# Retention followed by a gated feed-forward: Y, S and the next A in one block on TensorE, even pairs prepared sooner

## The chip, the core and the metric

The kernel runs on one core of one Trainium2 chip. The metric is the time of one execution on the device in microseconds (us). Before the change it is 210.73 us, the median of 4 runs (210.41 to 212.07).

## The reference

A linear recurrence ("retention") with a decay for each head feeds a two-layer network whose middle function is h·cos(h):

```python
# batch 4, heads 8, sequence 768, head size 64; gamma[h] = 1 - 2**(-5-h)
for t in range(S):
    state = gamma * state + outer(k[:, :, t], v[:, :, t])     # 64 x 64 per batch and head
    y[:, :, t] = (1 / sqrt(D)) * q[:, :, t] @ state
x = y as 3072 rows of 512
h = x @ w_in            # 512 x 2048
out = (h * cos(h)) @ w_out   # 2048 x 512, out is 3072 x 512 float32
```

## The kernel before

**Pairs and groups.** The sequence is cut into 6 chunks of 128 positions, and two batch rows are worked on together. One chunk of two batch rows is a "pair" `p`, numbered 0 to 11; pairs 0 to 5 are the first two batch rows, pairs 6 to 11 the other two, and at pairs 0 and 6 the state starts anew. Two neighbouring pairs make a "group" `g` of 512 rows, numbered 0 to 5, on which the feed-forward works.

**Steps of a pair.**

- Loads: six DMAs of 256 KB (q, k and v for each of the two batch rows, float32), issued from GpSimd's queue (L131), with some early ones on SyncE's.
- Conversion to bf16 with the decay multiplied in: q and v on GpSimd (`conv_q` L181, `conv_v` L186), k as a plain copy on ScalarE (`conv_k` L192). The function `ahead(p)` emits all three.
- Transposes of q and k: for the first pairs on TensorE (`stage_t`), from pair 4 on by two DMA transposes on SyncE's queue (`stage_t_dma` L218), written into the tile `qkt`.
- A (`stage_a` L235): for each batch row 8 matmuls of 64 rows by 128 columns, so 16 a pair; the products k·q go into four PSUM banks, two for each batch row.
- M (`stage_m` L244): VectorE multiplies these four banks by the causal mask and writes the tile `am`, four instructions, two for each batch row.
- Y (`half_y`, one call for each batch row): matmuls of the state from before (`stb`, L257; left out at pairs 0 and 6) and of `vs` with `am` (L262) into one bank for each batch row. ScalarE copies each bank into `xt` (L266).
- S (`stage_s` L279): 16 matmuls that add the pair's own part to the state in the PSUM tile `st_ps`. Then two copies bring the state to SBUF as `stb` for the next pair (L284; on VectorE from pair 4 on). Pairs 5 and 11 have no S.

**Steps of a group.** F is `unit_f` (L310): 4 matmuls of 128x512 against `w_in` give one of 16 slices of h; ScalarE takes the cosine (L299, tile `cosb`), VectorE multiplies it in (L303, tile `gt`), and then the bank is free. O is `unit_o` (L334): 4 of the 16 matmuls against `w_out` for one 128-row slice of the output; after the fourth such part ScalarE copies the bank to `ob` (L341) and SyncE's queue sends it out (L342).

**What sets the order.** Everything is emitted in an order that is written out by hand, and each engine executes its own instructions in that order. PSUM has 8 banks: one is `st_ps`, the other seven are handed out by `Banks`. A small model (`Clock`) guesses when each bank is free, and the bank with the earliest guess is taken; the actual wait is by semaphore. From group 2 on, the loop over `g` has 16 slots `s`; each has one F of group `g` and, for `g` above 2, one O of group `g - 1`. In group 2 six O of group 1 are interleaved (slots 0, 2, 4, 6, 8, 10). Beside these, a slot emits steps of the pairs of group `g + 1`, with r = s mod 8 and p = 2(g+1) for the first eight slots and 2(g+1)+1 for the others: the conversions of pair p+1 at r = 0, its DMA transposes at r = 1, A of pair p with half of M at r = 2, the other half of M at r = 3, and at r = 6 Y, S and the state copies of pair p and the loads of pair p+3.

The tiles `qk`, `vs` and `qkt` have three buffers each (pair modulo 3), `stb`, `am`, `xt` and `gt` have two.

Of the kernel before, what the change touches and what calls it, by code (L numbers as in the profile page):

```python
# [47 lines left out]
def kernel(  # L48
# [9 lines left out]
    nc = tc.nc  # L58
    B, H, S, D = q.shape
    C = 128  # L60
    NC = S // C
# [5 lines left out]
    NP = B // 2 * NC  # L67
    NG = NP // 2
# [15 lines left out]
    clk = Clock()  # L84
# [41 lines left out]
    def load(eng, p, names):  # L126
        bp, c = divmod(p, NC)
        for n in names:
            t, src = SRC[n[0]]
            b = int(n[1])  # L130
            eng.dma_start(  # L131
                out=t[SLOT[p]][b],
                in_=src[2 * bp + b, :, ds(c * C, C)].rearrange("h t d -> t h d"))
# [45 lines left out]
    def conv_q(p, eng, bs=(0, 1)):  # L179
        for b in bs:  # L180
            eng.tensor_tensor(out=qk[p % NB][:, b, 0], in0=qf[SLOT[p]][b],  # L181
                              in1=bc(gq, p % NC), op=ALU.mult)

    def conv_v(p, eng, bs=(0, 1), g=None):
        for b in bs:
            eng.tensor_tensor(out=vs[p % NB][:, b], in0=vf[SLOT[p]][b],  # L186
                              in1=bc(gk if g is None else g, p % NC), op=ALU.mult)

    def conv_k(p, on_act):
        for b in range(2):  # L190
            if on_act:
                nc.scalar.copy(out=qk[p % NB][:, b, 1], in_=kf[SLOT[p]][b])  # L192
                clk.run("act", 0.6)
            else:
                nc.vector.tensor_copy(out=qk[p % NB][:, b, 1], in_=kf[SLOT[p]][b])
# [19 lines left out]
    def stage_t_dma(p):  # L215
        n = p % NB
        for b in range(2):
            nc.sync.dma_start_transpose(  # L218
                out=qkt[n][:, b].rearrange("p w a t -> p (w a) t"),
                in_=qk[n][:, b].rearrange("p w h d -> p (w h d)"))  # L220

    def qt(n, b, a):
        return qkt[n][:, b, 0, a, :]

    def kt(n, b, a):
        return qkt[n][:, b, 1, a, :]

    def stage_a(p, b):
        n = p % NB
        bk = [banks.take(), banks.take()]  # L230
        ap = [t.rearrange("p (a t) -> p a t", a=HP) for t in bk]
        for a in range(HP):
            for j in range(2):
                po = 64 * j
                nc.tensor.matmul(ap[j][:, a, :], lhsT=kt(n, b, a)[po : po + 64, :],  # L235
                                 rhs=qt(n, b, a)[po : po + 64, :],
                                 tile_position=(po, 0))
        clk.run("pe", 0.3)
        return b, bk, ap, clk.pe

    def stage_m(p, item, parts=(0, 1)):
        b, bk, ap, done = item
        for j in parts:
            nc.vector.tensor_tensor(  # L244
                out=am[p % 2][b][j], in0=ap[j],
                in1=mask.unsqueeze(1).to_broadcast([128, HP, 128]), op=ALU.mult)
            banks.give(bk[j], clk.run("dve", 0.64, done + 0.1))

    def half_y(p, b):
        c = p % NC  # L250
        n = p % NB
        bank = banks.take()
        yp = bank.rearrange("p (a t) -> p a t", a=HP)
        for a in range(HP):
            if c > 0:
                for j in range(2):
                    nc.tensor.matmul(  # L257
                        yp[ts(j, 64), a, :], lhsT=stb[p % 2][:, b, a, ts(j, 64)],
                        rhs=qt(n, b, a), start=True, stop=False,
                        skip_group_check=True)  # L260
            for j in range(2):
                nc.tensor.matmul(  # L262
                    yp[ts(j, 64), a, :], lhsT=vs[n][:, b, 2 * a + j, :],
                    rhs=am[p % 2][b][j][:, a, :], start=(c == 0), stop=True,
                    skip_group_check=True)
        nc.scalar.copy(out=xt[(p // 2) % 2][:, :, ts(2 * (p % 2) + b, C)], in_=yp)  # L266
        clk.run("pe", 0.5)
        banks.give(bank, clk.run("act", 0.6, clk.pe + 0.1))

    def stage_s(p, copy_st):  # L270
        c = p % NC
        n = p % NB
        if c == NC - 1:
            return
        for b in range(2):
            for a in range(HP):
                for j in range(2):
                    h = 2 * a + j
                    nc.tensor.matmul(  # L279
                        st_ps[ts(j, 64), b, a, :], lhsT=qk[n][:, b, 1, h, :],  # L280
                        rhs=vs[n][:, b, h, :], start=(c == 0 and b == 0 and a == 0),
                        stop=True, skip_group_check=True)
        for j in range(2):
            copy_st(out=stb[(p + 1) % 2][ts(j, 64), :, :, ts(j, 64)], in_=st_ps[ts(j, 64)])  # L284
            clk.run("act" if copy_st == nc.scalar.copy else "dve", 0.65, clk.pe + 0.3)
        clk.run("pe", 0.25)

    def stage_y(p, copy_st=nc.vector.tensor_copy):
        for b in range(2):
            half_y(p, b)  # L290
        stage_s(p, copy_st)
# [15 lines left out]
    def unit_f(g, f):  # L307
        bank = banks.take()
        for i in range(KIN):
            nc.tensor.matmul(bank, lhsT=w_in_t(i, f), rhs=xt[g % 2][:, i, :],  # L310
                             start=(i == 0), stop=(i == KIN - 1))
        banks.give(bank, act(bank, gt[g % 2][:, f, :]))
# [16 lines left out]
    def unit_o(g, j, part):  # L329
        if part == 0:  # L330
            o_bank[j] = banks.take()
        bank = o_bank[j]
        for f in range(4 * part, 4 * part + 4):
            nc.tensor.matmul(bank, lhsT=gt[g % 2][:, f, ts(j, 128)], rhs=w_out_sb[:, f, :],  # L334
                             start=(f == 0), stop=(f == KOUT - 1))
        clk.run("pe", 0.87)
        if part == 3:
            o = ob[j % 4]
            bp, c = divmod(2 * g + j // 2, NC)
            dst = out[ds((2 * bp + j % 2) * S + c * C, C), :]  # L340
            nc.scalar.copy(out=o, in_=bank)  # L341
            nc.sync.dma_start(out=dst, in_=o)  # L342
            banks.give(bank, clk.run("act", 0.6, clk.pe + 0.1))
# [27 lines left out]
    def attend(p):  # L371
        for it in [stage_a(p, b) for b in range(2)]:
            stage_m(p, it)
# [36 lines left out]
    stage_t(1, 1)  # L410
    warm(1)
    stage_s(0, nc.scalar.copy)
    a10 = stage_a(1, 0)
    stage_m(1, a10)
# [6 lines left out]
    pair_f(0, 0, (0,))  # L421
    half_y(1, 1)
    stage_s(1, nc.scalar.copy)
    pair_f(0, 0, (1,))
    pair_f(1, 0)
# [56 lines left out]
    def ahead(p):  # L482
        if p < NP:
            conv_q(p, nc.gpsimd)
            conv_k(p, True)
            conv_v(p, nc.gpsimd)

    def later(p):
        stage_y(p)
        n = 8 if p == 4 else p + 3 if p > 5 else NP  # L490
        if n < NP:
            load(nc.gpsimd, n, ("q0", "k0", "q1", "k1", "v0", "v1"))

    def o_units(g, a, b):
        for u in range(a, b):
            unit_o(g, *divmod(u, 4))

    o_units(1, 0, 2)
    attend(4)
    stage_t_dma(6)  # L500
    o_units(1, 2, 6)
    later(4)
    attend(5)
    o_units(1, 6, 10)
    later(5)

    for g in range(2, NG + 1):
        for s in range(16):
            hf, r = divmod(s, 8)
            p = 2 * (g + 1) + hf  # L510
            if g == 2 and s % 2 == 0 and s < 12:
                unit_o(1, *divmod(10 + s // 2, 4))
            if g < NG:
                unit_f(g, s)
            if g > 2:
                if g < NG or s < 12:
                    unit_o(g - 1, *divmod(s, 4))
                elif s == 12:
                    last_o(g - 1, 3)
            if p < NP:  # L520
                if r == 0:
                    ahead(p + 1)
                elif r == 1:
                    if p + 1 < NP:
                        stage_t_dma(p + 1)
                elif r == 2:
                    todo = [stage_a(p, b) for b in range(2)]
                    stage_m(p, todo[0])
                elif r == 3:
                    stage_m(p, todo[1])  # L530
                elif r == 6:
                    later(p)


# [28 lines left out]
```

## Time and profile before

| What | Value |
|---|---|
| median of 4 runs | 210.73 us (210.41 to 212.07) |
| the profiled execution | 210.85 us, of which the span from first to last instruction is 209.1 us |
| TensorE matmul busy | 199.8 us, 1648 instructions |
| VectorE busy | 113.9 us, 189 instructions |
| ScalarE busy | 113.1 us, 189 instructions |
| GpSimd busy | 101.8 us, 117 instructions |
| granted TensorE clock | 1.000 |
| DMA | 33.83 MB, mean 162 GB/s |

The profile names engines PE (TensorE matmuls), PEld (TensorE weight loads), DVE (VectorE), ACT (ScalarE), POOL (GpSimd) and SP (SyncE); a q behind the name means the engine's queue of instructions that do no arithmetic, DMA issues among them. A row of the timeline or of the chain gives a start in us from the span's beginning, a length in us, the engine, the line in the kernel, the operation and how many instructions were merged into the row. Some matmul records are missing from a trace, so a row may say x15 or x3 where the program has 16 or 4; spaces of time between starts are then the better measure than counts. "Busy" on PE is the time from a matmul's start to its modelled end, and neighbouring matmuls overlap.

### The profile page before, as it was taken

Reading aid. Unit: us, or ns where it says so; the run is one execution under the profiler, and the core shown is the slowest. Engines: PE = TensorE matmul, PEld = TensorE weight load, DVE = VectorE, ACT = ScalarE, POOL = GpSimd, SP = SyncE. Lnnn points to the kernel's source line nnn. Section 1 sums busy time; section 2 is a strip of 40 time slices with the busy share of each in tenths; the row PEclk is TensorE's granted clock in tenths of the full one; section 3 lists DMA queues with packets and bytes.
Section 4 is the critical chain, followed back from the end, with each engine's and each line's share of the span. In section 5 each row is a group of like instructions: output and inputs, shape, how many; then the busy total and the mean of one; then the engine's idle time right before and its main releaser. Section 6 shows DMA issues by size and latency. Waiting matters only on the chain.

```text
span 209.1 us, 4209 instructions
## 1 busy us (share of the span) xinstructions
PE 199.8 (96%) x1648; PEld 115.6 (55%) x1671; DVE 113.9 (54%) x189; ACT 113.1 (54%) x189; POOL 101.8 (49%) x117
## 2 busy tenths in 40 slices
PE   7679999999999999999999999999999999999993
PEld 3258854558897555555545445545545444444452
DVE  5674885542967472968874575565565233333000
ACT  6386874237898227477744744734544654553120
POOL 7998238399999999999994130000000000000000
PEclk9999999999999999999999999999999999999999
DMA  6999999999999999959999991141101101110212
GB/s 153 332 251 207 216 252 288 330 261 285 274 301 240 262 263 269 223 183 215 149 250 110 137 202 50 56 100 50 53 0 50 50 3 50 50 52 6 97 63 87
DMA packets 37604, 33.83 MB, mean 162 GB/s; under 512 B 27792, under 2 KB 30096, under 8 KB 37584
## 3 DMA queue, kind: packets, MB, share of 16 engines
q0 software_dynamic: 7728, 20.71, 39.0%
q1 hardware_dynamic: 29712, 12.75, 27.9%
q8 instruction: 13, 0.21, 0.4%
q10 hardware_dynamic: 144, 0.10, 0.1%
q14 instruction: 7, 0.06, 0.1%
HBM read 27.26 MB, written 6.29 MB: 160 GB/s over the span
## 4 chain that ended last, share of the span: by engine, by line
PE 91%; DMA 3%; ACT 2%; issue 1%; SPq 1%; DVE 0%; DVEq 0%; ACTq 0%
PE bank L334 38%; PE bank L310 30%; PE bank L321 10%; DMA qf<-in_q_dram 3%; PE bank L235 3%; PE bank L257 3%; PE bank L262 3%; PE bank L351 2%; PE st_ps L279 1%; PE bank L208 1%; SPq L131 1%; ACT qk L391 1%; PE bank L368 1%; ACT qk L192 0%; ACT xt L266 0%
## 5 line engine op out<-in xcount | busy, mean ns | idle before, releaser
L303 DVE TENSOR_TENSOR gt<-bank,cosb 128x512 bf16<-128x512 f32 x96 | 65.2, 689 | 62.7 <-ACT cosb L299 62.5
L299 ACT ACTIVATE cosb<-bank,halfpi 128x512 bf16<-128x512 f32 x96 | 65.5, 687 | 50.5 <-PE bank L310 45.7
L334 PE MATMUL bank<-w_out_sb,gt 128*128 128x512 bf16 x358 | 88.4, 379 | 0.7 <-issue 0.3
L310 PE MATMUL bank<-xt,w_in 128*128 128x512 bf16 x277 | 70.4, 380 | 1.2 <-issue 0.9
L334 PEld LDWEIGHTS <-gt 128*128 128x128 bf16 x368 | 35.5, 98 | 41.2
L310 PEld LDWEIGHTS <-w_in 128*128 128x128 bf16 x288 | 31.8, 114 | 28.4
L244 DVE TENSOR_TENSOR am<-bank,mask 128x512 bf16<-128x512 f32 x48 | 30.3, 681 | 1.6 <-PE bank L235 1.5
L186 POOL TENSOR_TENSOR vs<-vf,gk 128x512 bf16<-128x512 f32 x22 | 22.5, 1045 | 3.5 <-DMA vf<-in_v_dram 3.5
L341 ACT COPY ob<-bank 128x512 f32<-128x512 f32 x23 | 13.4, 586 | 19.3 <-PE bank L334 19.2
L131 POOL DMA_DIRECT2D vf<-in_v_dram x23 | 20.3, 887 | 4.9 <-DMA w_out_sb<-in_moe_w_out_dram 4.9
L181 POOL TENSOR_TENSOR qk<-qf,gq 128x512 bf16<-128x512 f32 x18 | 18.5, 1050 | 7.7 <-issue 4.8
L321 PE MATMUL bank<-xt,w_in 128*128 128x256 bf16 x192 | 22.0, 273 | 0.0
L131 POOL DMA_DIRECT2D kf<-in_k_dram x23 | 20.6, 897 | 2.1 <-DMA w_out_sb<-in_moe_w_out_dram 1.2
L321 PEld LDWEIGHTS <-w_in 128*128 128x128 bf16 x192 | 20.7, 114 | 0.5
L192 ACT CAST qk<-kf 128x512 bf16<-128x512 f32 x24 | 13.7, 613 | 8.1 <-DMA kf<-in_k_dram 8.1
L266 ACT CAST xt<-bank 128x512 bf16<-128x512 f32 x24 | 13.0, 586 | 7.5 <-PE bank L262 7.5
L131 POOL DMA_DIRECT2D qf<-in_q_dram x17 | 15.3, 901 | 1.6 <-DMA w_in<-in_moe_w_in_dram 1.6
L262 PE MATMUL bank<-am,vs 128*64 128x128 bf16 x192 | 11.9, 220 | 0.6 <-POOL vs L186 0.6
L257 PEld LDWEIGHTS <-stb 128*64 128x64 bf16 x160 | 8.7, 109 | 4.4 <-issue 3.3
L262 PEld LDWEIGHTS <-vs 128*64 128x64 bf16 x192 | 10.0, 110 | 2.0 <-POOL vs L186 1.6
L284 DVE CAST stb<-st_ps 64x512 bf16<-64x512 f32 x12 | 8.2, 687 | 4.9 <-PE st_ps L279 4.7
L257 PE MATMUL bank<-qkt,stb 128*64 128x128 bf16 x160 | 10.7, 223 | 0.0
(39 smaller groups left out, 76.4 us busy)
## 6 DMA issues: line engine op xcount, KB each, us to landing
kf<-in_k_dram POOLq DMA_DIRECT2D x23, 256.0 KB, 5.9
vf<-in_v_dram POOLq DMA_DIRECT2D x23, 256.0 KB, 6.2
out_dram<-ob SPq DMA_DIRECT2D x23, 256.0 KB, 3.0
qf<-in_q_dram POOLq DMA_DIRECT2D x17, 256.0 KB, 5.9
w_in<-in_moe_w_in_dram POOLq DMA_DIRECT2D x4, 512.0 KB, 8.3
w_out_sb<-in_moe_w_out_dram POOLq DMA_DIRECT2D x4, 512.0 KB, 12.5
qf<-in_q_dram SPq DMA_DIRECT2D x7, 256.0 KB, 7.8
kf<-in_k_dram SPq DMA_DIRECT2D x1, 256.0 KB, 5.0
```

The source lines that it names most:

```text
L131: eng.dma_start(out=t[SLOT[p]][b], in_=src[2 * bp + b, :, ds(c * C, C)].rearrange("h t d -> t h d"))
L181: eng.tensor_tensor(out=qk[p % NB][:, b, 0], in0=qf[SLOT[p]][b], in1=bc(gq, p % NC), op=ALU.mult)
L186: eng.tensor_tensor(out=vs[p % NB][:, b], in0=vf[SLOT[p]][b], in1=bc(gk if g is None else g, p % NC), op=ALU.mult)
L192: nc.scalar.copy(out=qk[p % NB][:, b, 1], in_=kf[SLOT[p]][b])
L244: nc.vector.tensor_tensor(out=am[p % 2][b][j], in0=ap[j], in1=mask.unsqueeze(1).to_broadcast([128, HP, 128]), op=ALU.mult)
L257: nc.tensor.matmul(yp[ts(j, 64), a, :], lhsT=stb[p % 2][:, b, a, ts(j, 64)], rhs=qt(n, b, a), start=True, stop=False, skip_group_check=True)
L262: nc.tensor.matmul(yp[ts(j, 64), a, :], lhsT=vs[n][:, b, 2 * a + j, :], rhs=am[p % 2][b][j][:, a, :], start=(c == 0), stop=True, skip_grou ...
L299: nc.scalar.activation(out=cb, in_=bank, func=AF.Sin, bias=halfpi)
L303: nc.vector.tensor_tensor(out=out, in0=bank, in1=cb, op=ALU.mult)
L310: nc.tensor.matmul(bank, lhsT=w_in_t(i, f), rhs=xt[g % 2][:, i, :], start=(i == 0), stop=(i == KIN - 1))
L321: nc.tensor.matmul(bank[:, ts(e, 256)], lhsT=w_in_t(i, f + e), rhs=xt[g % 2][:, i, ts(hf, 256)], start=(i == 0 and e == 0), stop=(i == KIN ...
L334: nc.tensor.matmul(bank, lhsT=gt[g % 2][:, f, ts(j, 128)], rhs=w_out_sb[:, f, :], start=(f == 0), stop=(f == KOUT - 1))
```

## The change

From pair 5 on, A no longer has a place of its own. A new function `stage_ya(p)` emits Y and S of pair p, then A of pair p+1 directly behind them, then the half of M for the first batch row. The second half of M and the two state copies are put on a list, `late`; each slot takes one step from the list after its F and O. So the order on VectorE around a block is: first half of M, one multiply of F, second half of M, one multiply of F, the state copies. Until now the state copies followed S at once and stood ahead of both halves of M.

In the loop, `stage_ya(2(g+1))` stands in slot 10 and `stage_ya(2(g+1)+1)` in slot 14. Before, Y and S stood in slots 6 and 14, and A in slots 2 and 10. The conversions and DMA transposes of the even pairs move from slots 8 and 9 to slots 6 and 7. The loads of pairs 9 to 11 are issued one conversion later on GpSimd's queue: behind the conversions of pairs 8, 9 and 10 and no longer ahead of them. Two more O of group 1 stand ahead of the loop (its slots 0, 3, 6 and 9 have the remaining four). Behind Y of pair 4 the order on TensorE is as before; its state copies come behind the mask multiplications of pair 5. The number of instructions is the same on every engine.

```diff
@@ stage_s
+        clk.run("pe", 0.25)
+        if copy_st is not None:
+            state_out(p, copy_st)
+
+    def state_out(p, copy_st):
+        if p % NC == NC - 1:
+            return
         for j in range(2):
             copy_st(out=stb[(p + 1) % 2][ts(j, 64), :, :, ts(j, 64)], in_=st_ps[ts(j, 64)])
-            clk.run("act" if copy_st == nc.scalar.copy else "dve", 0.65, clk.pe + 0.3)
-        clk.run("pe", 0.25)
+            clk.run("act" if copy_st == nc.scalar.copy else "dve", 0.65, clk.pe + 0.1)
...
-    def later(p):
-        stage_y(p)
-        n = 8 if p == 4 else p + 3 if p > 5 else NP
-        if n < NP:
-            load(nc.gpsimd, n, ("q0", "k0", "q1", "k1", "v0", "v1"))
...
+    def fetch(p):
+        load(nc.gpsimd, p, ("q0", "k0", "q1", "k1", "v0", "v1"))
+    late = []
+    def then(*steps):
+        late.extend(steps)
+    def next_step():
+        if late:
+            late.pop(0)()
+    def stage_ya(p):
+        stage_y(p, None)
+        if p + 1 < NP:
+            todo = [stage_a(p + 1, b) for b in range(2)]
+            stage_m(p + 1, todo[0])
+            then(lambda: stage_m(p + 1, todo[1]))
+        then(lambda: state_out(p, nc.vector.tensor_copy))
...
     o_units(1, 2, 6)
-    later(4)
-    attend(5)
-    o_units(1, 6, 10)
-    later(5)
+    stage_ya(4)
+    next_step()
+    fetch(8)
+    o_units(1, 6, 7)
+    next_step()
+    o_units(1, 7, 12)
+    stage_ya(5)

     for g in range(2, NG + 1):
+        p = 2 * (g + 1)
         for s in range(16):
-            hf, r = divmod(s, 8)
-            p = 2 * (g + 1) + hf
-            if g == 2 and s % 2 == 0 and s < 12:
-                unit_o(1, *divmod(10 + s // 2, 4))
+            if g == 2 and s in (0, 3, 6, 9):
+                unit_o(1, 3, s // 3)
             if g < NG:
                 unit_f(g, s)
...
-            if p < NP:
-                if r == 0:
-                    ahead(p + 1)
-                elif r == 1:
-                    if p + 1 < NP:
-                        stage_t_dma(p + 1)
-                elif r == 2:
-                    todo = [stage_a(p, b) for b in range(2)]
-                    stage_m(p, todo[0])
-                elif r == 3:
-                    stage_m(p, todo[1])
-                elif r == 6:
-                    later(p)
+            next_step()
+            if g == NG:
+                continue
+            if s == 0 and p + 1 < NP:
+                ahead(p + 1)
+                if 9 < p + 2 < NP:
+                    fetch(p + 2)
+            elif s == 1 and p + 1 < NP:
+                stage_t_dma(p + 1)
+            elif s == 6 and p + 2 < NP:
+                ahead(p + 2)
+                fetch(p + 3)
+            elif s == 7 and p + 2 < NP:
+                stage_t_dma(p + 2)
+            elif s == 10 and p < NP:
+                stage_ya(p)
+            elif s == 14 and p < NP:
+                stage_ya(p + 1)
```

## The prediction

> **What bounds the kernel.** I read the page first, then the chain that ended last in order of time, then the timelines of VectorE, GpSimd and SyncE around group 2.
>
> ```profile
> PE 199.8 (96%) x1648; PEld 115.6 (55%) x1671; DVE 113.9 (54%) x189; ACT 113.1 (54%) x189; POOL 101.8 (49%) x117
> ...
> PE 91%; DMA 3%; ACT 2%; issue 1%; SPq 1%; DVE 0%; DVEq 0%; ACTq 0%
> ```
>
> TensorE is busy for 96% of the span and holds 91% of the chain; from about 16 us on nothing else stands in it. What the change can win is therefore TensorE time, and any new wait of TensorE adds in full. What a block of small matmuls costs there is read off the chain, as the distance from its start to the start of a later row, less the F and O between:
>
> ```profile
> 71.76 0.18 PE bank L257 x2
> ...
> 72.78 0.25 PE st_ps L279 x16
> 73.03 0.55 PE bank L235 x16
> 73.74 3.40 PE bank L334 x15
> 77.14 0.18 PE bank L257 x2
> ...
> 121.99 0.55 PE bank L235 x16
> ...
> 123.53 0.86 PE bank L334 x4
> ...
> 129.57 0.18 PE bank L257 x2
> ...
> 131.83 0.86 PE bank L334 x4
> ```
>
> One F or O takes 0.863 (the spacing of the 0.86 rows). A alone (121.99 to 123.53, one F inside): 1.54 - 0.86 = 0.67. Y and S (129.57 to 131.83, one F inside): 2.26 - 0.86 = 1.39. The first block above is Y, S and A of pairs 4 and 5, which already stand together: 71.76 to 77.14 holds four O (16 matmuls, one record is missing), so 5.38 - 3.45 = 1.93. Apart they cost 2.06, together 1.93: joining saves 0.12 to 0.13.
>
> **The gain on TensorE.** A of pairs 6 to 11 is joined to the block before it, six times; A of pair 5 was joined already. 6 x 0.12 = 0.7 us. This is small because the joined block still changes from the 128x64 shape of S to the 64x128 shape of A. Bounds: nothing, if that change costs what the two changes to the full shape did; at most what lies above A's bare row, 6 x (0.67 - 0.43) = 1.4 (16 matmuls in two halves side by side, first to last start 0.41). I take 0.7, since it comes from the same sequence in the same trace.
>
> The Trainium skill, TensorEngine Tiling (Array Packing), section Tiling Modes, says that a change of tiling mode drains TensorE; a joined A saves one of four changes. If each cost a whole 0.17 us, an estimate from the drain that TensorE: Matmul & The Clock Gate gives in Part 2, the six would be worth 1.0; the rows show less, and the rows decide.
>
> **What VectorE now has between two blocks.** In group 2 the slots are short: there is one F in each, and no O behind slot 9. Y of pair 7 (slot 14) reads the state that S of pair 6 (slot 10) leaves, and the copies of it to `stb` are now behind both halves of the mask. The durations:
>
> ```profile
> 89.80 1.40 DVE L284 CAST stb<-st_ps 64x512 bf16<-64x512 f32 x2
> ...
> 95.41 0.69 DVE L303 TENSOR_TENSOR gt<-bank,cosb 128x512 bf16<-128x512 f32 x1 [0.38 <-ACT cosb L299]
> 96.01 1.28 DVE L244 TENSOR_TENSOR am<-bank,mask 128x512 bf16<-128x512 f32 x2
> 97.21 0.68 DVE L303 TENSOR_TENSOR gt<-bank,cosb 128x512 bf16<-128x512 f32 x1
> 97.81 1.28 DVE L244 TENSOR_TENSOR am<-bank,mask 128x512 bf16<-128x512 f32 x2
> ```
>
> Back to back, a multiply takes 0.60 from start to start, two mask halves 1.20, two state copies 1.40. Before, the copies were done at 91.2 while Y of pair 7 began at 98.68: hidden by four F and an A. That cover is what the change takes away. Let T be the end of F in slot 10. In the rows, its multiply starts 1.0 after that (last matmul start 94.18, multiply 95.41). Pair 6 has no state term, so its Y and S cost 0.93 (88.43 to 90.24 in the chain, less one F, is 0.95); with A the block is 0.93 + 0.67 - 0.12 = 1.48, and A's first half is done before the multiply is. So VectorE:
>
> - multiply of slot 10: T+1.0 to 1.6; first half of M: to 2.8
> - F of slot 11 runs from T+1.5 to 2.35; by the same lag its multiply starts at 3.35, to 3.95
> - second half of M: to 5.15; multiply of slot 12 (its cosine is ready at about 4.2): to 5.75
> - state copies: to 7.15
>
> TensorE: after the block, four F of 0.863, so Y of pair 7 would begin at T + 1.48 + 3.45 + 0.10 = T+5.03. It waits until T+7.15 and a little for the signal: **2.2 us of standing still**, nothing else being left to do on TensorE ahead of it. Queued behind the waiting Y are S, A of pair 8 and F of slot 15; VectorE and ScalarE catch up meanwhile and nobody else is late. Below: if the signal and the gap ahead of slot 11's multiply vanish, 1.6; above: if a cosine comes late behind the copies to `xt`, 2.8.
>
> In groups 3 and 4 a slot has an O as well, 1.73 us: the copies end at about T+7.6 and the next Y comes at T + 1.93 + 4 x 1.73 = T+8.8. No wait, 1.2 in hand. Ahead of the loop, the copies of pair 4 end at about 77.7 (VectorE: four mask operations from 73.7, then 1.4), and Y of pair 5, now behind six O, comes at 78.8. No wait either.
>
> **The steps moved sooner.** For pair 8, GpSimd's part (four conversions, 2 x 2.05, against six issues of 0.88 that now follow) runs at 83.1 to 87.2 instead of 88.5 to 92.5. ScalarE's two k copies (1.13) go from slot 8 to slot 6, which delays a cosine by 1.1 us; the slots until 10 take that up (0.86 a slot against 0.60 for a cosine back to back). The transposes on SyncE then issue at about 90.6 and 91.9; an output DMA waits behind them, which nobody needs. They are due earlier: A of pair 8 came in slot 2 of group 3, and now follows Y of pair 7. With six O ahead of Y of pair 5, group 2 starts at 80.4 and T is 93.3 (15 units of 0.863), so A of pair 8 is due at T+8.4 = 101.7, eleven us after its issue. What transposes take:
>
> ```profile
> L218 SPq DMA_TRANSPOSE qkt<-qk x2: 1233/1404/1576, 93.3 to 94.7; - x2
> ...
> DMA to landing us min/median/max: 5.9/8.1/10.3
> ...
> L218 SPq DMA_TRANSPOSE qkt<-qk x2: 1237/2897/4557, 103.1 to 104.5; - x2
> ...
> DMA to landing us min/median/max: 13.7/15.3/16.9
> ```
>
> Those issued before a load landed in 2.7 to 6.4; these two pairs were issued 0.8 and 1.3 us into a load's six issues and took up to 10.3 and 16.9. The new ones fall 3.4 us into the load of pair 9 (87.2 to 92.4), with half of it moved. From both ends: landing at 95 costs nothing, landing at 91.9 + 16.9 = 108.8 costs 7. I take the nearer row, 10.3: 102.2, so 0.3 late, and count 0.1 to 0.3. Pair 10's transposes have some 15 us before A, and only the 16.9 row would hurt, by about 2.
>
> **Banks.** A's second half for pair 8 uses the bank of Y's first half, whose ScalarE copy (0.59) ends about when it is needed: 0 to 0.3, taken as 0. F of slot 11 the same.
>
> **Sum.** 210.85 - 0.7 + 2.2 + 0.1 = 212.45 for an execution like the profiled one. The median lies 0.12 below that execution, so 212.3.
>
> **The rivals.**
>
> 1. *The state copies hold Y of pair 7* and nothing else is late: 212.0 to 213.0. For it: an order that is fixed by the program, and rows that add up. Chance 0.58.
> 2. *The transposes land late too.* As above, pair 8 (or 10) waits 1 to 7 us more: 213.3 to 219, most likely 215. For it: the 13.7 to 16.9 row. Against: no load was still moving from before when these start, as there was at 103. Chance 0.20. TensorE: Matmul & The Clock Gate, section Why this matters for your kernels, warns of idle gaps over about 3 us, behind which the clock is halved for a while; the longest idle of TensorE's rows here after its first matmul is 0.83 us at a clock of 1.00, so no row of this case shows it.
> 3. *The wait is not there, or mostly not* (the other side). It decides at T+5.0: were the copies done by then, only the joining is left, 210.1; with half of the wait, 211.2. It needs VectorE to get through 2.2 us less work between the two Y than the rows say. Against: each term is a row of the same operation in the same slots. Chance 0.17.
> 4. *The joining is worth its upper bound* and there is no wait: 209.4. Chance 0.05.
>
> **How the numbers follow.** About 0.5% (1.05 us) can be told from no change. Faster by that means below 209.7: rival 4 and a little of 3, 0.06. Within it, up to 211.8: most of 3 and the short end of 1, 0.20. Slower: 0.74. The range must leave out at most 0.2: it goes from 210.1 (rival 3 without a wait) to 215.5 (half of rival 2).
>
> **What would show it.** In the profile after, the chain or the waits should name the state copy L291 as what Y of pair 7 (L257) waited for, some 2 us at about 98 to 100.5, and no such wait in groups 3 and 4. The six blocks should cost 1.9 each (1.5 and 1.7 for pairs 6 and 5). In the same window VectorE's rows should be back to back from the second half of M to the copies. A wait of L235 on a DMA at about 102 would speak for rival 2. I am wrong if TensorE's rows run through 98 to 101 without a gap, or if a gap of over 1 us stands anywhere else.

## The result and the profile after

The changed kernel takes 213.74 us (median of 40 runs, 211.71 to 232.57) against 211.38 us for the kernel before (61 runs, 210.34 upward). The ratio is 1.010, with a 95% interval of 1.008 to 1.0119: slower by 1.0%, some 2.1 us; the forecast was 0.75%. Executions more than 1.5% above the fastest one of their kernel are left out of this ratio and of the ratios below. The 30 that remain of the changed kernel lie on two levels, which is explained below. The profiled execution took 212.86 us, its span is 211.1 us, 2.0 more than before.

The page of the changed kernel, the lines that answer to the first two shown of before:

```profile
PE 199.9 (95%) x1650; PEld 115.8 (55%) x1671; DVE 114.0 (54%) x189; ACT 113.4 (54%) x189; POOL 102.0 (48%) x117
...
PE 74%; DMA 17%; ACT 2%; DVE 2%; issue 1%; SPq 1%; POOL 1%; DVEq 0%; POOLq 0%; ACTq 0%
```

TensorE has the same work in a longer span, and the chain, which was 91% TensorE, now runs for 17% over DMAs. VectorE's timeline around the two blocks of group 2 (start, length, engine, line, operation, in brackets the idle time before):

```profile
94.42 0.69 DVE L309 TENSOR_TENSOR gt<-bank,cosb 128x512 bf16<-128x512 f32 x1 [0.17 <-ACT cosb L305]
95.03 1.28 DVE L244 TENSOR_TENSOR am<-bank,mask 128x512 bf16<-128x512 f32 x2
96.78 0.69 DVE L309 TENSOR_TENSOR gt<-bank,cosb 128x512 bf16<-128x512 f32 x1 [0.47 <-ACT cosb L305]
97.39 1.28 DVE L244 TENSOR_TENSOR am<-bank,mask 128x512 bf16<-128x512 f32 x2
98.58 0.68 DVE L309 TENSOR_TENSOR gt<-bank,cosb 128x512 bf16<-128x512 f32 x1
99.18 1.40 DVE L291 CAST stb<-st_ps 64x512 bf16<-64x512 f32 x2
```

And TensorE's timeline beside it:

```profile
96.72 1.89 PE L316 MATMUL bank<-xt,w_in 128*128 128x512 bf16 x8
99.91 0.24 PE L257 MATMUL bank<-qkt,stb 128*64 128x128 bf16 x1 [1.30 <-DVE stb L291]
100.63 0.24 PE L257 MATMUL bank<-qkt,stb 128*64 128x128 bf16 x1 [0.48 <-DVE stb L291]
```

The last F ends at 98.4; one matmul of Y runs when the first of the two state copies is done, the rest at 100.63, when the second is. The block of Y, S and A at this place costs 4.00 (from the start of the last F matmul ahead of it to the start of the first one behind it, less the 0.22 between two F matmuls), where the same block costs 1.91 in the later groups: a wait of 2.09. There the state copies hold nothing up: in group 3 they end at 129.9 and the next Y starts at 131.2.

The second new wait is in group 3. The chain in order of time (start, length):

```profile
116.34 3.67 DMA qf<-in_q_dram x2
120.01 13.18 DMA qkt<-qk
133.19 0.04 issue
133.23 0.40 PE bank L235 x8
```

The second DMA transpose of pair 10, issued at 120.01 in the middle of the loads of pair 11, landed after 13.2 us, and A of pair 10 stood waiting for it; its block cost 2.38, 0.47 more than 1.91. So for this execution: six joins at -0.12, the two waits 2.09 and 0.47, 1.84 in all. The rest up to 2.0 had already come up ahead of group 2, in the first 72 us: the joined block of pair 4, whose order is the old one, starts at 71.93 and not at 71.76.

### The profile page after: what moved, and what is told of

It reads as the page before. It is cut to its first block, busy times and chain, and to the rows that moved or that the text cites. A ratio compares the mean times of both kernels' runs of the same rounds, so it can differ in the third digit from the quotient of the medians.

```text
span 211.1 us, 4202 instructions
## 1 busy us (share of the span) xinstructions
PE 199.9 (95%) x1650; PEld 115.8 (55%) x1671; DVE 114.0 (54%) x189; ACT 113.4 (54%) x189; POOL 102.0 (48%) x117
## 4 chain that ended last, share of the span: by engine, by line
PE 74%; DMA 17%; ACT 2%; DVE 2%; issue 1%; SPq 1%; POOL 1%; DVEq 0%; POOLq 0%; ACTq 0%
PE bank L340 31%; PE bank L316 22%; PE bank L327 10%; DMA qf<-in_q_dram 6%; DMA qkt<-qk 6%; DMA vf<-in_v_dram 4%; PE bank L235 2%; PE bank L257 2%; PE bank L262 2%; PE bank L357 2%; PE bank L208 1%; ACT qk L397 1%; SPq L131 1%; PE st_ps L279 1%; ACT xt L266 1%
## 5 line engine op out<-in xcount | busy, mean ns | idle before, releaser
L244 DVE TENSOR_TENSOR am<-bank,mask 128x512 bf16<-128x512 f32 x48 | 30.4, 682 | 11.1 <-PE bank L235 8.0
L186 POOL TENSOR_TENSOR vs<-vf,gk 128x512 bf16<-128x512 f32 x22 | 22.5, 1045 | 16.5 <-DMA vf<-in_v_dram 9.1
L347 ACT COPY ob<-bank 128x512 f32<-128x512 f32 x23 | 13.4, 588 | 22.5 <-PE bank L340 22.5
L181 POOL TENSOR_TENSOR qk<-qf,gq 128x512 bf16<-128x512 f32 x18 | 18.6, 1049 | 5.8 <-issue 2.6
L235 PE MATMUL bank<-qkt 64*128 64x128 bf16 x192 | 8.1, 218 | 1.0 <-DVE qkt L198 0.4
## 6 DMA issues: line engine op xcount, KB each, us to landing
w_out_sb<-in_moe_w_out_dram POOLq DMA_DIRECT2D x4, 512.0 KB, 12.7
```

The lines of the kernel that those rows point to most:

```text
L244: nc.vector.tensor_tensor(out=am[p % 2][b][j], in0=ap[j], in1=mask.unsqueeze(1).to_broadcast([128, HP, 128]), op=ALU.mult)
```

## The experiments

The experiments are told in the order in which they were made. Where nothing else is said, each edit is made to the changed kernel.

**State copies on ScalarE.**

```diff
-        stage_y(p, None)
+        stage_y(p, nc.scalar.copy)
...
-        then(lambda: state_out(p, nc.vector.tensor_copy))
```

> The state copies go to ScalarE directly behind S, nothing else changes. Theory (Y of pair 7 waits 2.1 us because two state copies come last in VectorE's queue): the wait shrinks to at most 0.1 to 0.2 us, the joined block of pairs 7 and 8 costs 1.9 to 2.1 us and not 4.0, and the time falls by about 2.0 to 210.9. Rival (the time went to late DMA transposes): the block keeps most of its 4.0 us, time 212 or more. Second theory (a wait of 2 us sometimes lowers the granted clock behind it, which makes the median 1 us longer than the profiled execution): without the wait no execution has a mean granted clock of about 0.99, and the median stands at the profiled time; without such an effect the times spread as after the change.

Measured: lowest 210.35, median 214.06, ratio 0.9999 (0.996 to 1.0038). The lowest value fell by 1.36 against the change's 211.71, and the wait on the copies is gone in the trace; but the median did not fall, and the profiled execution is one of seven long ones (of 13), 216.68. TensorE's timeline and the windows (busy times of PE, PEld, DVE, ACT and POOL, then the granted clock, DMA share, GB/s):

```profile
100.27 0.40 PE L235 MATMUL bank<-qkt 64*128 64x128 bf16 x8 [0.87 <-DMA qkt<-qk]
103.73 0.61 PE L235 MATMUL bank<-qkt 64*128 64x128 bf16 x8 [3.07 <-DMA qkt<-qk]
...
102.00:104.00 2.00, 0.27 (x6) 0.27 (x8) 0.00 (x0) 0.00 (x0) 1.04 (x2) 0.50 0.56 179
104.00:106.00 2.00, 1.78 (x12) 0.71 (x8) 0.00 (x0) 0.00 (x0) 2.00 (x3) 0.50 0.03 8
106.00:108.00 2.00, 2.00 (x6) 0.73 (x5) 1.07 (x2) 0.77 (x2) 2.00 (x3) 0.50 0.62 162
```

Now A of pair 8 waits in two pieces for its transposes, which landed 10.1 and 12.1 us after their issue, and from about 102 on, inside that wait, TensorE's clock is granted at 0.50. So removing the first wait lets another one out that stood behind it. The second theory of the expectation stays open here: the six executions in the ratio have mean clocks of 0.998 and more, the seven long ones of 0.956 to 0.992, but in the long one that was profiled the clock falls inside the wait on the transposes, so the two cannot be told apart here.

**State copies on VectorE at once.**

```diff
-        stage_y(p, None)
+        stage_y(p)
...
-        then(lambda: state_out(p, nc.vector.tensor_copy))
```

> The state copies stay on VectorE but go back to their old place directly behind S, ahead of both mask halves. By the sum VectorE reaches the last mask half at T+6.0 where Y's second half is due at T+5.5: a wait of about 0.5 us stays, the block costs 2.4, the time is about 211.3. If only the amount of VectorE work between the two Y counts and not its order, the wait stays at 2 us and the time at 212.9. If the state copies alone were the cause and the mask has slack, the time is 210.8.

Measured: lowest 210.71, median 211.49, ratio 0.9995 (0.9959 to 1.003). In the profile Y's first half runs through and its second half is held up by the mask (L244): its first matmul with `am` starts at 98.58, the next only at 99.10. That is the 0.5 of the sum. Another 0.4 is a wait of A on the transposes, which the expectation did not have: the block cost 2.8 and not 2.4. The order on VectorE, not only the amount of work, makes the wait.

**Loads ahead of the conversions.**

```diff
-                ahead(p + 1)
                 if 9 < p + 2 < NP:
                     fetch(p + 2)
+                ahead(p + 1)
...
-                ahead(p + 2)
                 fetch(p + 3)
+                ahead(p + 2)
```

> The loads of pairs 9 to 11 are again issued ahead of the conversions of pairs 8 to 10. Theory: the transposes of pair 10 then no longer start in the middle of a load and land in 3 to 6 us instead of 13.2, so A of pair 10 does not wait: 0.5 us less than the change, about 212.4, with the 2.1 us wait at pair 7 untouched. Rival (their landing is set by how much the DMA engines have to move in all): they land as late as before, and the time stays at 212.9.

Measured: lowest 211.71, median 220.55, ratio 1.0051 (0.9999 to 1.0103). The transposes of pair 10 landed in 2.7 us, as the theory had it. But the load of pair 9 (82.9 to 88.2) now began beside the transposes of pair 7, and those of pair 8, issued at 90.7 and 92.1, met the load of pair 10 (from 92.2 on) and took 10.2 and 18.6 us, so that A of pair 8 waited 8.1 us in the profiled execution (222.29). The collision was moved to a place where A follows sooner: a miss, and it speaks for the theory that which load a transpose meets is what matters, against the rival.

**Both of these edits** (state copies on ScalarE, loads ahead):

> Both edits: state copies on ScalarE directly behind S, and the loads ahead of the conversions. If the two waits are the whole loss, only the joining is left: 0.6 to 0.7 us under the kernel before, about 210.2 for an execution like the profiled one, and all executions at a granted clock of 1.00. If the joining gains nothing, it equals the kernel before, 210.85.

Measured: median 225.52 (223.85 to 230.97), ratio 1.0631 (1.0572 to 1.069). Far from what was expected. The issues of the transposes of pair 8 and their landing (issue time min/median/max in ns, then us to landing):

```profile
L218 SPq DMA_TRANSPOSE qkt<-qk x2: 1232/6612/11991, 91.0 to 92.4; - x2
...
DMA to landing us min/median/max: 18.0/22.1/26.3
```

The loads meet the transposes as in the experiment before, A of pair 8 waits 4.35 and 9.30 us for its two halves, and the block of pairs 7 and 8 costs 16 us. Why the transposes took still longer here than there was not followed.

**Loads and transposes kept apart.** GpSimd reads eight columns of the transposed tile ahead of the loads; that makes it wait until the transposes have landed.

```diff
+    def landed(p):
+        n = p % NB
+        nc.gpsimd.tensor_tensor(out=seen, in0=qkt[n][:, 0, 0, 0, :8],
+                                in1=qkt[n][:, 1, 0, 0, :8], op=ALU.mult)
...
             if s == 0 and p + 1 < NP:
                 ahead(p + 1)
-                if 9 < p + 2 < NP:
-                    fetch(p + 2)
-            elif s == 1 and p + 1 < NP:
+            elif s == (4 if g == 3 else 1) and p + 1 < NP:
                 stage_t_dma(p + 1)
             elif s == 6 and p + 2 < NP:
                 ahead(p + 2)
-                fetch(p + 3)
             elif s == 7 and p + 2 < NP:
                 stage_t_dma(p + 2)
+                landed(p + 2)
+                fetch(p + 3)
+                if g == 2:
+                    fetch(p + 4)
```

> The change, with loads and DMA transposes kept from running at the same time: GpSimd issues the loads of pairs 9 and 10 only after the transposes of pair 8 have landed, those of pair 11 only after the transposes of pair 10, and the transposes of pair 9 are issued three slots later. VectorE's order stays, so Y of pair 7 waits 2.1 us. Theory (what goes beyond the forecast is transposes landing late): they land in 2.7 to 3 us each, A waits nowhere, and the time is 211.7, the lowest value that the change itself has shown, in nearly all executions. Rival (the 2.1 us wait by itself lowers the granted clock in a part of the executions): times stay spread, with a second level about 1.7 us above the first, and mean clocks of about 0.99.

Measured: lowest 211.83, median 212.26, ratio 1.0071 (1.0034 to 1.0108). The transposes of pair 8 landed in 3.9 and 4.4 us, all later ones in 2.7 to 2.8, and A waits for none. The block of pairs 7 and 8 still costs 4.00, as in the change. Eight of twelve executions lie between 211.8 and 212.6, but 213.3, 213.5 and 214.5 are there too, at mean clocks of 0.989 to 0.992 (and one of 233.2), which the rival has and the theory has not. This is the forecast's own case, with one wait alone, and it came out at 0.71% against the forecast's 0.75%. That it came so near is in part luck: 3 of the 11 executions in the ratio have the lower clock here, 6 of 11 in the repeat below, which came out at 0.84%.

**Apart, and the state copies on ScalarE.**

> As before it, and the state copies on ScalarE directly behind S. Both waits are gone and only the joining is left: 0.7 us under the lowest value of the kernel before (210.34), so 209.6, and nearly all executions within 0.5 us. If the joining is worth nothing, 210.3; if the transposes still land late, 212 and more in a part of the executions.

Measured: lowest 209.61, median 209.81 (to 212.15), ratio 0.9972 (0.9948 to 0.9997). ScalarE's and VectorE's timelines, then the landing of pair 8's transposes:

```profile
95.04 1.19 ACT L292 CAST stb<-st_ps 64x512 bf16<-64x512 f32 x2
```

```profile
97.58 1.28 DVE L245 TENSOR_TENSOR am<-bank,mask 128x512 bf16<-128x512 f32 x2
```

```profile
DMA to landing us min/median/max: 3.9/4.1/4.3
```

The copies are done at 96.2, the mask at 98.9, and Y of pair 7 (first matmul at 98.35) finds what it needs; its block costs 1.94. The lowest value is 0.70 below the lowest of the kernel before in the same call (210.31): the size forecast for the joining, though this version differs from the kernel before in more than the joining. It is faster than both kernels, by 0.3% against the one before and by 0.5% in the repeat below.

**The same with A split off**: `then(lambda: attend(p + 1))` in place of A behind S.

> As the one before, but A (with both halves of M) is issued one slot later, behind the next F and O, for all six pairs: Y and S, then F and O, then A. This measures the joining by itself. By the rows of before it costs 0.12 us for each of six blocks, 0.7 us more than the joined one: 210.3. Rival: the change of shape between S and A costs as much as the two changes that it replaces, then both are equal. In the profile A alone should cost 0.66 and Y with S 1.38, against 1.92 together.

Measured: lowest 211.60, median 211.94, ratio 1.0062 (1.0038 to 1.0086): 2.0 slower than the joined version, not 0.7. The blocks themselves came out as expected: 0.65 to 0.68 for A alone and 1.36 for Y and S, against 1.91 together. But A of pair 7, one F later, brings the mask later, and TensorE's timeline has

```profile
100.98 0.22 PE L263 MATMUL bank<-am,vs 128*64 128x128 bf16 x1 [0.38 <-DVE am L245]
```

so that the block of Y and S of pair 7 costs 1.15 more (2.51 against 1.36). Six joins at 0.12 and 1.15 are 1.87 of the 2.0. As a measurement of the joining alone by time, the run is spoiled by this wait; the blocks in its trace measure it.

**Apart, with the state copies of pair 6 done twice.**

```diff
-        then(lambda: state_out(p, nc.vector.tensor_copy))
+        then(lambda: [state_out(p, nc.vector.tensor_copy) for _ in range(2 if p == 6 else 1)])
```

> The first of these four, with the two state copies of pair 6 done twice on VectorE (the same values once more), 1.40 us more ahead of Y of pair 7: a wait of 3.5 us. If a wait only costs its own length, the time is 213.1. If a wait of over about 3 us also lowers the granted clock, the profile shows a clock of 0.50 for some microseconds behind it, and the time is 214 to 215.

Measured: lowest 213.29, median 215.95, ratio 1.0216 (1.0166 to 1.0265). The lowest is 1.46 above that of the version with single copies: in that execution, at a mean clock of 1.000, the longer wait cost its own length and no more. Four others lie 1.4 to 3.0 above that lowest value, at mean clocks of 0.982 to 0.992. The profiled one was a long one (233.22), with transposes of pair 6 that took 22.5 us, but in it the wait at Y of pair 7 can be seen (the window's columns as above):

```profile
119.17 0.24 PE L258 MATMUL bank<-qkt,stb 128*64 128x128 bf16 x1 [2.74 <-DVE stb L292]
...
118.00:120.00 2.00, 0.34 (x5) 0.21 (x7) 1.91 (x4) 0.00 (x0) 2.00 (x3) 1.00 0.97 301
120.00:122.00 2.00, 2.00 (x63) 1.94 (x63) 1.29 (x3) 1.07 (x2) 2.00 (x3) 0.75 0.99 281
122.00:124.00 2.00, 1.78 (x10) 0.70 (x7) 1.17 (x2) 0.00 (x0) 2.00 (x3) 0.50 1.00 311
124.00:126.00 2.00, 2.00 (x10) 0.92 (x9) 1.15 (x2) 1.47 (x3) 1.99 (x4) 0.90 0.90 262
```

No transposes are late at this place. The wait ends at 119.9, 3.5 us after Y was due; from about 121 the clock is 0.50 for some 3.4 us (half of the second window, all of the third, a fifth of the fourth).

**Three of them once more, on one chip.** First the change itself:

> The change itself, on the same chip and beside the next kernel, so that the two distributions can be compared. Theory (a wait of 2.1 us in every execution, and late transposes in most): lowest value 211.7, median 1 to 2 us above the next kernel's, a tail over 215. Rival (the earlier difference between the two came from different chips): both have the same median within 0.3 us.

Measured: lowest 213.16, median 214.55 of only six executions, two of them over 230, ratio 1.0121 (1.0059 to 1.0183): too few to tell the theory from the rival. The profiled execution, 215.41 at a mean clock of 0.989, is of use all the same. Y of pair 7 waits as in the first profile (1.29 and 0.48 us ahead of its first two matmuls), the transposes of pair 8 landed in 5.0 and 5.6 us and A does not wait for them, and right behind the block the clock falls: 0.75 in the window from 102 to 104, 0.90 in that from 106 to 108, and between them

```profile
104.00:106.00 2.00, 2.00 (x18) 0.98 (x13) 1.29 (x2) 0.00 (x0) 1.53 (x2) 0.50 0.87 270
```

Then the version with loads and transposes apart:

> The change with loads and transposes kept apart, once more: lowest 211.8, median 212.0 to 212.3, and transposes of pairs 8 and 10 that land in under 4.5 us. By the rival theory the same median as the kernel before it in this call.

Measured: lowest 211.81, median 213.27, ratio 1.0084 (1.0042 to 1.0125). The median is 1 us above the expectation. Five executions lie at 211.8 to 212.1, at mean clocks of 0.997 to 1.000, six at 213.2 to 214.8, at 0.989 to 0.992. The profiled one is of the second kind, 213.49, and its transposes landed in 2.7 to 4.3 us, so they are not why. Its windows, and below them those of the execution profiled in the first run of the same kernel (211.88):

```profile
98.00:100.00 2.00, 0.42 (x2) 0.11 (x1) 1.97 (x4) 0.73 (x2) 2.00 (x3) 1.00 0.77 215
100.00:102.00 2.00, 1.80 (x53) 1.74 (x55) 1.43 (x3) 1.12 (x2) 2.00 (x3) 0.75 0.96 283
102.00:104.00 2.00, 2.00 (x19) 1.00 (x16) 1.29 (x2) 0.05 (x1) 2.00 (x3) 0.50 0.98 303
104.00:106.00 2.00, 2.00 (x10) 0.94 (x9) 0.65 (x2) 1.20 (x2) 2.00 (x4) 0.90 0.96 281
```

```profile
98.00:100.00 2.00, 0.33 (x2) 0.11 (x1) 1.97 (x4) 0.69 (x1) 2.00 (x3) 1.00 0.79 205
100.00:102.00 2.00, 1.89 (x64) 1.75 (x65) 1.54 (x4) 1.07 (x2) 2.00 (x3) 1.00 0.92 283
102.00:104.00 2.00, 1.95 (x9) 1.04 (x11) 1.35 (x3) 0.81 (x2) 2.00 (x4) 1.00 0.97 289
```

The same kernel, the same idle stretch at 98 to 100 (0.42 and 0.33 of 2.00 busy); in the one the clock is then halved for some 3.4 us (half of the second window, all of the third, a fifth of the fourth), in the other not. The difference of the two executions is 1.6. Last, the version without either wait:

> The version with both waits removed, once more, for its time against the kernel before and against the change: lowest 209.6, median 209.8, 0.4 to 0.5% under the kernel before.

Measured: lowest 209.62, median 209.89, highest 211.38, ratio 0.9946 (0.9916 to 0.9975). Its profile has no window around the two blocks with a clock under 1.00.

## Why the forecast was too small

**The joining**, -0.7: right. From start to start, less the F and O between, as in the prediction, a joined block costs 1.94 in group 4 after, against 0.67 and 1.38 before: 0.11 a block. The time without the waits is 0.70 under the kernel before, lowest against lowest.

**The wait of Y of pair 7**, 2.2: right, 2.09 in the profile. Its place, its releaser and VectorE's sequence are those of the prediction, the gap of 0.47 ahead of slot 11's multiply included, and with the copies on ScalarE it is gone from the trace, with the copies ahead of the mask on VectorE 0.5 of it is left. Lowest value against lowest value the change costs 211.71 - 210.34 = 1.37, which is 2.09 less 0.72.

**What the wait costs behind it**: this term was missing, and it is the step that failed first. I priced the wait at its own length, 2.2, and put the clock behind it at nothing. In 13 of the 30 executions in the ratio the mean granted clock is 0.989 to 0.992; their median is 213.84, that of the 17 others, at 0.997 to 1.000, is 212.35. The profiles of the change on the second occasion and of the version with nothing late but this wait show why: 2.1 us of standing still are in some executions followed by some 3.4 us at half clock, worth about 1.5. Thirteen times 1.5 in 30 is 0.65 on average; with the 1.37 it makes 2.0 of the 2.1 us measured. All versions with this wait of 2.1 us together have 27 of 61 such executions in their ratios. The versions without it (state copies on ScalarE, at once, apart on ScalarE twice, and A split off) have none of 50, and the kernel before none of the 61 measured beside the experiments: there the mean clock is 0.997 or more.

The prediction set the clock aside because the longest idle of TensorE's rows before was 0.83 us and because the Trainium skill, in TensorE: Matmul & The Clock Gate, section Why this matters for your kernels, puts the bound at about 3 us. The measurement decides: 2.1 us were enough in somewhat under half of the executions. In the execution that was profiled first, the one by which the sum was to be tested, the clock stayed at 1.00; what the sum lacks there is 0.4 of the transposes, below, and the 0.17 by which the execution was late at 72 us.

**The transposes**, 0.1 to 0.3: too small in size, and at another place. For pair 8 they landed in 8.8 and 9.0 us and were just in time, because the wait ahead of them lasted 2.1 us: with the state copies on ScalarE A waits for them. (A landing 10.3 after an issue at 91.9 is 0.5 behind 101.7 and not the 0.3 that I wrote; nothing hangs on it.) For pair 10 I had counted 15 us of slack and a cost only for a landing of 16.9; it had 12.7 (issued at 120.0, due at 132.8). What I did not follow is GpSimd's queue behind the moved load: the conversion of v of pair 9 waited 5.2 us for its load, which landed 8.7 and 8.9 us after its issue beside the transposes of pair 8 (4.6 to 4.8 in the version with both kept apart),

```profile
99.47 2.04 POOL L186 TENSOR_TENSOR vs<-vf,gk 128x512 bf16<-128x512 f32 x2 [5.19 <-DMA vf<-in_v_dram]
```

so that the loads of pairs 10 and 11 came that much later, and the last one started at 116.3, two us ahead of pair 10's transposes. Their landing took 13.2 and cost 0.47 in the profile. The profile of before already had such a row: two loads of v, issued at 105.3 and 106.2 beside late transposes, landed after 16.0 and 16.1 us, and GpSimd waited 3.5 us for them. Whether late transposes also make the tail above 215 is not shown: the one execution of the changed kernel there that was profiled (215.41) lost 1.5 to the clock, and its only wait on transposes was 0.48 ahead of A of pair 5.

**The rivals.** The second one (late transposes) is true beside the first, not in its place, and small in the execution profiled: 0.47, not 1 to 7 us. The third and fourth (no wait) are excluded by the trace of the change; the fourth's bound of 1.4 for the joining is excluded by the blocks, too.

Not settled: why the clock falls after the same 2.1 us in one execution and not in another, and how much of the tail of the kernel before comes from its own transposes among loads. A kernel that fills the wait with other matmuls was not run.

## What to carry to other kernels

Moving a copy behind other work on an engine with spare time is free only up to the first reader in the shortest stretch of the program: go through the slots one by one, since here groups 3 and 4 had 1.3 us in hand and group 2, in the same loop, was 2.1 short. Where TensorE is busy almost all the time, as here, a wait of 2 us should be priced at its length and, by these runs, a chance of a little under one half of 1.5 more for the clock. Transposes by DMA should be given a time in which no large load is in flight; where an order cannot promise that, a small read of the transposed tile ahead of the load does.

## What was not expected of the hardware

- The two DMA transposes of a pair (128x1024 values each) landed in 2.7 to 4.6 us from pair 8 on in the versions that keep them apart from the loads, and in up to 26.3 us among loads of six times 256 KB; the loads are slowed as well, from 4.6 to 4.8 us for v to 8.7 to 8.9 in the profile of the change. Keeping them apart made GpSimd wait 5 to 10 us for each landing in the profiles of ordinary length, and TensorE not at all.
- TensorE's granted clock fell to 0.50 for some 3.4 us behind a wait of 2.1 us in somewhat under half of the executions, and behind one of 3.5 us in the one that was profiled. In the profiles of the version without such a wait it stays at 1.00 there.
